# Scatter products of hops 2 to 7 as four 128x32 matrices a tile, and a table entry's low half moved one block later in the source

## The chip, the cores and the metric

One core of one Trainium2 chip runs the kernel. The metric is device time in microseconds (us) of an execution; the kernel before was timed in 3 runs with a median of 3949.62 us (3941.75 to 3951.11).

## What is computed

A graph has 10000 nodes with 128 features and 160000 random edges `src -> dst`. Seven times ("hops") each node takes the sum of its in-neighbours' features, scaled by `deg_inv_sqrt` at both ends. The eight stages of each node's features then go through a small attention block, and one row per node comes out. Cut to what matters here:

```python
h = x
toks = [x]
for _ in range(7):
    msg = h[src] * deg_inv_sqrt[src, None] * deg_inv_sqrt[dst, None]
    h = segment_sum(msg, dst, N)
    toks.append(h)
tok = stack(toks, axis=1)                    # (N, 8, D)
out = attention_readout(tok)                 # layer norm, one head, residual, softmax readout
```

## The kernel before, in words

The nodes are cut into 79 tiles of 128. Features live in a table in SBUF, `tab`, as two float16 halves per entry (a high half, columns 0 to 127, and a low half that holds the rounding error, columns 128 to 255); there are two tables, read and written in turn. The first stage sorts the edges; hop 1 also builds, for each tile of target nodes, a matrix row `w` of zeros and ones in float8 that is stored in DRAM (`GSd`) and loaded again in each of hops 2 to 7.

Hops 2 to 7 (`run`, second part) each run over 79 blocks, one for a tile `t` of target nodes, and call `block`. A block works in three steps.

- **Gather** (`gather`, L608): the edges of a tile are sorted into 72 cells of up to 32 edges, one per tile of source nodes. For each cell a product of a 128x32 matrix (a quarter of TensorE's columns, `tile_position=(0, 32 * q)`) with a table tile of 256 columns picks the 32 source rows. Four such products stand side by side and fill 128 partitions; two such groups fill one PSUM tile `p`, so a block has 9 tiles `p` and 72 products.
- **Eviction** (L613 and L615): tiles `p` 0, 2, 4, 5 and 7 are copied to SBUF (`eb`, a ring of 14) by ScalarE (ACT), tiles 1, 3, 6 and 8 by VectorE (DVE). There are 6 buffers for `p`, so tile 6 waits for the eviction of tile 0.
- **Scatter** (`scat`, L583): for each half of an `eb` tile a product of a 128x128 matrix of `w` with 256 columns adds the edges' rows into `acc`, one row per target node. There are 18 in a block.

Edges that fit in no cell are fetched row by row with an indirect DMA that POOL issues (`fetch`, L544): `og` from the table's last tiles (`tabh`), `og` of the overflow (`tabd`). Their rows go into `acc` with two more wide products (`fetched`, L568; `Sov` is the overflow's matrix). In the first two blocks of a hop the overflow's product comes last (L597, "late"). The fetch for a block is issued two blocks ahead; the first of its two DMAs stands behind a one-column copy (L543) that waits for an eviction of the block's first tile.

Scatter lags behind gather: TensorE's order in a block is 72 gather products, the two L568 products, the last 4 scatter products of the block before, then the first 14 of this one. When the last scatter product of a block is done, `close` sums the two halves of `acc` on DVE (L599, `s`), and `fin` makes the next table's entry (`entries`: the high half on ACT, L644; the low half on DVE, L645; the largest value on DVE, L646), sends the entry's rows to DRAM for the later fetches (`rows`, L168 and L172, on SP's queue), and writes the token (`token_out`: scaled by POOL, L653; sent by SP, L655).

The code is written in program order, and a scheduler then sets the order of the instructions on each engine; waits are by semaphores. In hop 1, `block` runs with `first` set and adds the halves apart (L558, L559); the change does not reach it. The attention at the end runs from an order written out by hand and is the same in both kernels.

Of the kernel before, what the change touches and what calls it, by code (L numbers as in the profile page):

```python
# [13 lines left out]
ALU = mybir.AluOpType  # L14
X = mybir.AxisListType.X
# [4 lines left out]
NT = 79  # L20
NG = 18
NI = 1
# [25 lines left out]
class Hops:  # L48
# [91 lines left out]
    def spread(self, pp, m, out, tag="acc"):  # L140
        nc = self.nc
        pb = pp.tile([128, 512], F32, name="pb", tag=tag)[:, 0:1]
        nc.tensor.matmul(pb, self.ones32, m, start=True, stop=True)
        nc.vector.tensor_copy(out, pb)
# [401 lines left out]
        return o  # L546

    def block(self, t, w, tab, og, pend, lag, runs, first, evac, fin, lead=False, late=False, mid=None, ahead=None,
              after=None):

        nc, V, A, T, G = self.nc, self.nc.vector, self.nc.scalar, self.nc.tensor, self.nc.gpsimd
        acc = []

        def both(W, rows, start, ones):

            T.matmul(acc[0][:, :128 + ones], W, rows[:, 128:256 + ones], start=start, stop=False, skip_group_check=True)  # L558
            T.matmul(acc[0][:, :128], W, rows[:, :128], start=False, stop=False, skip_group_check=True)  # L559


        def fetched(i, start=False, stop=False):
            W = w[:, (NG + i) * 128:(NG + i + 1) * 128] if i < NI else self.Sov[:, t, :]
            if first:
                both(W, og[i], False, 0)
                T.matmul(acc[0][:, 128:129], W, self.ones16, start=False, stop=stop, skip_group_check=True)  # L566
                return
            T.matmul(acc[0][:, :256], W, og[i], start=start, stop=stop)  # L568

        def begin():  # L570
            acc.append(self.pacc.tile([128, 512], F32, name="acc", tag="acc"))
            for i in range(NI if late else NI + 1):
                fetched(i, start=i == 0)

        def scat(e, jj):
            if not acc:
                acc.append(self.pacc.tile([128, 512], F32, name="acc", tag="acc"))
            for j in range(e.shape[1]):
                J = 2 * jj + j
                if first:  # L580
                    both(w[:, J * 128:(J + 1) * 128], e[:, j], J == 0, 1)
                else:
                    T.matmul(acc[0][:, :256], w[:, J * 128:(J + 1) * 128], e[:, j, :256], start=False, stop=J == NG - 1 and not late)  # L583
                if first and J == 0 and not lead:
                    for i in range(NI):
                        fetched(i)

        def close():
            if first:
                if lead:  # L590
                    for i in range(NI):
                        fetched(i)
                fetched(NI, stop=True)
                fin(t, acc[0][:, :128], acc[0])
                return
            if late:
                T.matmul(acc[0][:, :256], self.Sov[:, t, :], og[NI], start=False, stop=True)  # L597
            s = self.fp.tile([128, 128], F32, name="s")
            V.tensor_reduce(s, acc[0][:, 0:256].rearrange("p (h d) -> p d h", h=2), axis=X, op=ALU.add)  # L599
            fin(t, s, acc[0])  # L600

        def gather(jj):
            n = min(2, NG - 2 * jj)
            p = self.pg.tile([128, 2, 2, 128], F32, name="p")
            for j in range(n):
                for q in range(4):
                    s = 4 * (2 * jj + j) + q
                    T.matmul(p[32 * q:32 * q + 32, j], w[:, NJ * 128 + s * CAP:NJ * 128 + (s + 1) * CAP], tab[:, s, :], start=True, stop=True)  # L608
            e = self.ebuf[self.eb_i % len(self.ebuf)]
            self.eb_i += 1  # L610
            pv = p[:, :n].rearrange("p j h d -> p j (h d)")
            if evac(jj):
                A.activation(e[:, :n, 0:256], pv, AF.Copy, scale=4.0)  # L613
            else:
                V.tensor_tensor(e[:, :n, 0:256], pv, self.four[:, :, None].to_broadcast([128, n, 256]), op=ALU.mult)  # L615
# [24 lines left out]

    def entries(self, t, s, i):

        c, new = self.c1[i][:, t:t + 1], self.tab[1 - i]
        self.nc.scalar.activation(new[:, t, 0:128], s, AF.Copy, scale=c)  # L644
        self.nc.vector.scalar_tensor_tensor(new[:, t, 128:256], s, c, new[:, t, 0:128], op0=ALU.mult, op1=ALU.subtract)  # L645
        self.nc.vector.tensor_reduce(self.mx[1 - i][:, t:t + 1], new[:, t, 0:128], axis=X, op=ALU.max, apply_absolute_value=True)  # L646

    def token_out(self, k, t, s, ct):
        r = self.fp.tile([128, 128], F32, name="r")
# [7 lines left out]
    def run(self, ctx, att, nhop=K):  # L657
        tc, nc, V, A, T, G = self.tc, self.nc, self.nc.vector, self.nc.scalar, self.nc.tensor, self.nc.gpsimd
        with ExitStack() as c:
# [35 lines left out]
            dsl, W = [[] for _ in quads], [[] for _ in quads]  # L695
# [30 lines left out]
        with ExitStack() as c:  # L726
# [11 lines left out]
            for k in range(2, nhop + 1):  # L738
                i = 1 - k % 2
# [20 lines left out]

                def fin(t, s, acc, k=k, ct=ct, last=last, i=i):
                    if not last:
                        self.entries(t, s, i)
                        self.rows(1 - i, self.tab[1 - i], t, t + 1, nc.sync)
                    self.token_out(k, t, s, ct)


                order = [*range(4 * NG, NT), *range(4 * NG)]
# [12 lines left out]
                for n, t in enumerate(order):  # L781
                    w = self.gsp.tile([128, (NJ + NG) * 128], F8, name="w")
                    nc.sync.dma_start(w, self.GSd[t])
                    if k == 2 and n == 20:
                        att.constants(c, self.pg.tile([128, 512], F32, name="aw", tag="p"), self.ident)
                    if last and 40 <= n < 40 + 8 * FIRST:
                        att.load((n - 40) // 8, (n % 8,))

                    after = pend.pop() if n == 1 else None
                    for _ in self.block(t, w, tab, og[n], pend, 2, (9,), False, lambda jj: jj in (0, 2, 4, 5, 7), fin, n == 0, n < 2,  # L790
                                        (lambda part, n=n: scale(part, n)) if n < 2 and not last else None,
                                        lambda after=None, n=n: ahead(n, after), after):
                        pass
                while pend:
                    pend.pop(0)()
# [578 lines left out]
```

## Time and profile before

| | us |
|---|---|
| median of 3 runs | 3949.62 |
| lowest, highest | 3941.75, 3951.11 |
| the profiled execution | 3958.33 |
| its span (first to last instruction) | 3956.4 |
| TensorE busy | 3707.2 |
| VectorE busy | 3165.6 |
| ScalarE busy | 2812.9 |
| POOL busy | 1689.8 |
| granted TensorE clock, mean | 0.974 |

Engines are named PE (TensorE's products), PEld (its weight loads), DVE, ACT, POOL and SP. "128*32" in a row is the matrix, "128x256" the moving operand. In a timeline each row is a run of equal instructions: start, duration, engine, line, what is written and read, how many, and in brackets how long the engine sat idle before and what ended it. In a chain each row is a stretch of the path that ended last.

### The profile page before, as it was taken

To read this page: it belongs to the slowest core of one execution; us is meant where nothing else is said; L and a number is where in the kernel's file an instruction comes from. 1 tells how busy PE (TensorE), PEld (TensorE's weight loads), DVE (VectorE), ACT (ScalarE), POOL (GpSimd) and SP (SyncE) were. 2 spreads that over 40 slices of the span, in tenths; PEclk is the share of its full clock that TensorE was granted. 3 is DMA by queue.
4 is the path that set the end of the run, shared out by engine and by line. 5 is a ranking of instruction groups with operands and counts; after the bars stand their busy time and mean duration, and the time that the engine had idled before them with its cause. 6 is when DMAs were issued, how large, how long until landed. Compare 5 with 4: busy or idle time off the path is not lost.

```text
span 3956.4 us, 174256 instructions
## 1 busy us (share of the span) xinstructions
PE 3707.2 (94%) x74141; PEld 2992.0 (76%) x74141; DVE 3165.6 (80%) x6888; ACT 2812.9 (71%) x6950; POOL 1689.8 (43%) x2221
## 2 busy tenths in 40 slices
PE   6787899999989999999999999999999998999997
PEld 4665677777768888888888788878878886777775
DVE  8998999998867777777777777777776664888888
ACT  6885577777776666766667677666765657888885
POOL 0000234333345665666566566656656662121111
PEclk8998899999999999999999999999999999999998
DMA  3100454545456666666666666666666653222220
GB/s 101 37 2 1 146 160 152 164 148 158 142 160 191 199 202 194 203 200 203 192 198 203 183 205 203 198 191 198 203 191 202 189 183 98 83 76 84 77 83 18
DMA packets 332729, 595.58 MB, mean 151 GB/s; under 512 B 57447, under 2 KB 215493, under 8 KB 326693
## 3 DMA queue, kind: packets, MB, share of 16 engines
q1 hardware_dynamic: 293989, 506.70, 40.6%
q0 software_dynamic: 35392, 72.55, 6.7%
q8 instruction: 580, 9.50, 1.0%
q10 hardware_dynamic: 2560, 5.12, 0.5%
q14 instruction: 208, 1.70, 0.2%
HBM read 455.49 MB, written 128.67 MB: 148 GB/s over the span
## 4 chain that ended last, share of the span: by engine, by line
PE 72%; DVE 16%; DMA 5%; ACT 3%; issue 2%; SPq 1%; another core or an unknown queue 0%; ACTq 0%; DVEq 0%; POOLq 0%
PE p L608 26%; PE acc L583 23%; PE acc L568 4%; PE pv L1018 4%; PE pu L1002 3%; DMA rb<-srow 2%; DVE o L219 2%; DVE w L532 2%; DVE oh L213 2%; DVE ux L226 2%; PE po L1037 2%; PE tb L449 2%; PE pt L992 2%; PE ps L1067 1%; ACT rs L347 1%
## 5 line engine op out<-in xcount | busy, mean ns | idle before, releaser
L613 ACT ACTIVATE eb<-p 128x512 f16<-128x512 f32 x3065 | 1636.7, 604 | 566.2 <-PE p L608 327.9
L615 DVE TENSOR_TENSOR eb<-p,four 128x512 f16<-128x512 f32 x1912 | 1232.0, 686 | 334.8 <-PE acc L583 201.3
L608 PE MATMUL p<-tab,w 128*32 128x256 f16 x39816 | 1296.2, 275 | 42.8 <-issue 15.3
L608 PEld LDWEIGHTS <-w 128*32 128x32 fp8e4 x39816 | 998.9, 96 | 231.6 <-issue 171.4
L583 PE MATMUL acc<-eb,w 128*128 128x256 f16 x8532 | 1013.6, 273 | 0.7 <-issue 0.7
L583 PEld LDWEIGHTS <-w 128*128 128x128 fp8e4 x8532 | 836.7, 98 | 99.9 <-issue 1.3
L544 POOL DMA_INDIRECT og<-tabh,oidx x553 | 626.1, 1132 | 662.3 <-DVE vi L487 388.3
L544 POOL DMA_INDIRECT og<-tabd,oidx x541 | 553.4, 1023 | 752.2 <-PE acc L566 311.8
L653 POOL TENSOR_SCALAR r<-s,ctok 128x128 f32<-128x128 f32 x474 | 294.9, 622 | 48.7 <-DVE s L599 31.1
L644 ACT ACTIVATE tab<-s,c 128x128 f16<-128x128 f32 x395 | 158.5, 401 | 204.0 <-DVE eb L615 167.7
L645 DVE SCALAR_TENSOR_TENSOR tab<-s,c,tab 128x128 f16<-128x128 f32 x395 | 138.9, 352 | 180.6 <-issue 168.8
L1107 POOL TENSOR_TENSOR p<-e,in 128x1024 f32<-128x1024 f32 (+1 forms) x40 | 76.5, 1913 | 447.0 <-DVE e L1106 447.0
L1059 ACT ACTIVATE junk<-tab 128x128 f32<-128x128 f32 x626 | 248.6, 402 | 8.4 <-SPq L1343 6.8
L347 ACT ACTIVATE rs<-iof,rb 128x128 fp8e4<-128x128 f32 x784 | 231.8, 389 | 0.3
L599 DVE TENSOR_REDUCE s<-acc 128x128 f32<-128x256 f32 x474 | 196.8, 415 | 24.8 <-PE acc L597 11.7
L558 PE MATMUL acc<-eb,w 128*128 128x129 f16 x1422 | 214.5, 225 | 1.8 <-ACT eb L613 1.7
L532 DVE TENSOR_TENSOR w<-dsl,iof 128x2432 fp8e4<-128x2432 f16 x79 | 211.9, 2683 | 0.8 <-PE acc L559 0.8
L559 PE MATMUL acc<-eb,w 128*128 128x128 f16 x1422 | 210.7, 222 | 0.0
L558 PEld LDWEIGHTS <-w 128*128 128x128 fp8e4 x1501 | 140.1, 98 | 65.8 <-issue 62.9
L543 POOL COPY og<-eb 128x1 f16<-128x1 f16 x452 | 84.1, 186 | 240.2 <-ACT eb L613 240.1
L1018 PEld LDWEIGHTS pv<-Wv,xT 128*64 128x64 f32 x2504 | 138.9, 137 | 44.7 <-ACT uT L1003 29.1
L1018 PE MATMUL pv<-Wv,xT 128*64 128x131 f32 x2504 | 163.6, 280 | 8.4 <-issue 4.6
(299 smaller groups left out, 5048.7 us busy)
## 6 DMA issues: line engine op xcount, KB each, us to landing
w<-gsd SPq DMA_DIRECT2D x474, 592.0 KB
gsd<-w SPq DMA_DIRECT2D x79, 592.0 KB
tok<-r SPq DMA_DIRECT2D x546, 64.0 KB
tab<-tok SPq DMA_DIRECT2D x273, 128.0 KB
tabd<-tab SPq DMA_DIRECT2D x396, 64.0 KB
ra<-srow SPq DMA_DIRECT2D x79, 320.0 KB
rb<-srow SPq DMA_DIRECT2D x79, 256.0 KB
og<-tabh,oidx POOLq DMA_INDIRECT x553
```

The lines of the kernel that those rows point to most:

```text
L347: A.activation(ro[:, j - a, i, :], self.iof, AF.Abs_reciprocal_sqrt, scale=2.0 ** 21, bias=rb[:, j - VP, i:i + 1], saturate=False)
L532: V.tensor_tensor(w[:, :NJ * 128].rearrange("p (j d) -> p j d", d=128), dsl[:, g, :, None].to_broadcast([128, NJ, 128]), self.iof1[:, None ...
L544: self.nc.gpsimd.indirect_dma_start(out=o, out_offset=None, in_=src[0] if i == NI else src[1], in_offset=bass.IndirectOffsetOnAxis(ap=self ...
L558: T.matmul(acc[0][:, :128 + ones], W, rows[:, 128:256 + ones], start=start, stop=False, skip_group_check=True)
L559: T.matmul(acc[0][:, :128], W, rows[:, :128], start=False, stop=False, skip_group_check=True)
L583: T.matmul(acc[0][:, :256], w[:, J * 128:(J + 1) * 128], e[:, j, :256], start=False, stop=J == NG - 1 and not late)
L608: T.matmul(p[32 * q:32 * q + 32, j], w[:, NJ * 128 + s * CAP:NJ * 128 + (s + 1) * CAP], tab[:, s, :], start=True, stop=True)
L613: A.activation(e[:, :n, 0:256], pv, AF.Copy, scale=4.0)
L615: V.tensor_tensor(e[:, :n, 0:256], pv, self.four[:, :, None].to_broadcast([128, n, 256]), op=ALU.mult)
L653: self.nc.gpsimd.tensor_scalar(r, s, ct[:, t:t + 1], None, op0=ALU.mult)
L1018: T.matmul(p[64 * h:64 * h + 64, u - us[0], :], S[i]["xT"][:, h * m + q, 64 * c:64 * c + 64], Wv, start=True, stop=True, tile_position=(0, ...
L1059: A.activation(j, S[i]["x"][:, g, :], AF.Square, bias=S[i]["x"][:, g, 0:1], scale=-1.0, accum_out=R[i % 6][:, 0, g:g + 1])
```

## The change

Two edits. In hops 2 to 7 each 128x128 product into `acc` (L568, L583, L597) becomes four products of 128x32, each with a quarter of the matrix's columns, the same 256 moving columns, and a quarter of `acc`'s partitions. And `entries` returns the making of the low half, of the largest value and of the rows' DMA as a function, which `fin` calls when the next block ends (for the last block of a hop, at once).

```diff
+            spread(W, og[i], start, stop)
+        def spread(W, rows, start, stop):
+            if not self.narrow:
+                T.matmul(acc[0][:, :256], W, rows, start=start, stop=stop)
+                return
+            for q in range(4):
+                T.matmul(acc[0][32 * q:32 * q + 32, :256], W[:, 32 * q:32 * q + 32], rows, start=start, stop=stop,
+                         tile_position=(0, 32 * q))
...
-                    T.matmul(acc[0][:, :256], w[:, J * 128:(J + 1) * 128], e[:, j, :256], start=False, stop=J == NG - 1 and not late)
+                    spread(w[:, J * 128:(J + 1) * 128], e[:, j, :256], False, J == NG - 1 and not late)
...
-                T.matmul(acc[0][:, :256], self.Sov[:, t, :], og[NI], start=False, stop=True)
+                spread(self.Sov[:, t, :], og[NI], False, True)
...
         self.nc.scalar.activation(new[:, t, 0:128], s, AF.Copy, scale=c)
-        self.nc.vector.scalar_tensor_tensor(new[:, t, 128:256], s, c, new[:, t, 0:128], op0=ALU.mult, op1=ALU.subtract)
-        self.nc.vector.tensor_reduce(self.mx[1 - i][:, t:t + 1], new[:, t, 0:128], axis=X, op=ALU.max, apply_absolute_value=True)
+        def rest():
+            self.nc.vector.scalar_tensor_tensor(new[:, t, 128:256], s, c, new[:, t, 0:128], op0=ALU.mult, op1=ALU.subtract)
+            self.nc.vector.tensor_reduce(self.mx[1 - i][:, t:t + 1], new[:, t, 0:128], axis=X, op=ALU.max, apply_absolute_value=True)
+            self.rows(1 - i, new, t, t + 1, self.nc.sync)
+        return rest
...
                     if not last:
-                        self.entries(t, s, i)
-                        self.rows(1 - i, self.tab[1 - i], t, t + 1, nc.sync)
+                        rest.append(self.entries(t, s, i))
                     self.token_out(k, t, s, ct)
+                    while len(rest) > (t != order[-1]):
+                        rest.pop(0)()
```

On TensorE, in the middle of a hop, these rows stood where gathers end and scatter begins (`og0` and `og1` are the fetched rows, `eb6` and `eb7` evicted tiles of the block before):

```order
L568 LDWEIGHTS w_48618
L568 MATMUL acc_48715<-og0_48376,w_48618 128x256
L568 LDWEIGHTS Sov_254
L568 MATMUL acc_48715<-og1_48379,Sov_254 128x256
L583 LDWEIGHTS w_48491
L583 MATMUL acc_48588<-eb6_24209,w_48491 128x256
```

In the change the first of these pairs is four, and so is each that follows (L576 is the new helper's product):

```order
L576 LDWEIGHTS w_63990
L576 MATMUL acc_64087<-og0_63628,w_63990 32x256
L576 LDWEIGHTS w_63990
L576 MATMUL acc_64087<-og0_63628,w_63990 32x256
L576 LDWEIGHTS w_63990
L576 MATMUL acc_64087<-og0_63628,w_63990 32x256
L576 LDWEIGHTS w_63990
L576 MATMUL acc_64087<-og0_63628,w_63990 32x256
```

A block has 152 pairs of load and product on TensorE now, where it had 92, all of them 128x32.

On VectorE, in a block in the middle of a hop, before:

```order
L615 TENSOR_TENSOR eb1_258<-p_60773,four_222 128x2x256
L615 TENSOR_TENSOR eb3_262<-p_60793,four_222 128x2x256
L599 TENSOR_REDUCE s_60810<-acc_60676 128x128
L645 SCALAR_TENSOR_TENSOR tab1_65<-s_60810,c10_24185,tab1_65 128x128
L646 TENSOR_REDUCE mx1_249<-tab1_65 128x1
```

And in the change, in the same place (L609 is the sum, L657 the low half, L658 the largest value):

```order
L625 TENSOR_TENSOR eb1_258<-p_77918,four_222 128x2x256
L625 TENSOR_TENSOR eb3_262<-p_77938,four_222 128x2x256
L609 TENSOR_REDUCE s_77973<-acc_77761 128x128
L657 SCALAR_TENSOR_TENSOR tab1_65<-s_77973,c10_24185,tab1_65 128x128
L658 TENSOR_REDUCE mx1_249<-tab1_65 128x1
```

The low half still reads the `s` that was summed just before it, of its own block: the scheduler has put it back where it stood, in all 395 cases.

On SP's queue, in the middle of a hop, before (`w` is the next matrix row, `tabd1` the entry's rows, `tok3` the token):

```order
L783 DMA w_37292<-gsd16_103 128x4736
L168 DMA tabd1_167<-tab1_65 128x256
L655 DMA tok3_68<-r_36894 128x128
L783 DMA w_37419<-gsd17_104 128x4736
L168 DMA tabd1_167<-tab1_65 128x256
```

And in the change:

```order
L799 DMA w_43397<-gsd16_103 128x4736
L670 DMA tok3_68<-r_42774 128x128
L168 DMA tabd1_167<-tab1_65 128x256
L799 DMA w_43584<-gsd17_104 128x4736
L670 DMA tok3_68<-r_42961 128x128
```

The entry's rows now stand behind the token, where they stood ahead of it.

More of the change, by code (lines that the diff above doesn't have):

```diff
@@ L548, in block @@
     def block(self, t, w, tab, og, pend, lag, runs, first, evac, fin, lead=False, late=False, mid=None, ahead=None,
-              after=None):
+              after=None, narrow=False):
         nc, V, A, T, G = self.nc, self.nc.vector, self.nc.scalar, self.nc.tensor, self.nc.gpsimd
@@ L567, in fetched @@
                 return
-            T.matmul(acc[0][:, :256], W, og[i], start=start, stop=stop)
+            spread(W, og[i], start, stop)
[6 more added lines that the diff above has]
+                         tile_position=(0, 32 * q))
         def begin():
+            self.narrow = narrow
             acc.append(self.pacc.tile([128, 512], F32, name="acc", tag="acc"))
@@ L762, in fin @@
                     if not last:
-                        self.entries(t, s, i)
-                        self.rows(1 - i, self.tab[1 - i], t, t + 1, nc.sync)
+                        rest.append(self.entries(t, s, i))
                     self.token_out(k, t, s, ct)
-                order = [*range(4 * NG, NT), *range(4 * NG)]
+                    while len(rest) > (t != order[-1]):
+                        rest.pop(0)()
+                order, rest = [*range(4 * NG, NT), *range(4 * NG)], []
                 og = [[None] * (NI + 1) for _ in order]
@@ L791, in run @@
                                         (lambda part, n=n: scale(part, n)) if n < 2 and not last else None,
-                                        lambda after=None, n=n: ahead(n, after), after):
+                                        lambda after=None, n=n: ahead(n, after), after, True):
                         pass
```

## The prediction

> **What bounds the kernel now.** I read the page's first part and its chain first, then the stretch that holds hops 2 to 7, then the chain in order of time inside one block, then the timeline of that block.
>
> ```profile
> PE 3707.2 (94%) x74141; PEld 2992.0 (76%) x74141; DVE 3165.6 (80%) x6888; ACT 2812.9 (71%) x6950; POOL 1689.8 (43%) x2221
> PE 72%; DVE 16%; DMA 5%; ACT 3%; issue 2%; SPq 1%; another core or an unknown queue 0%; ACTq 0%; DVEq 0%; POOLq 0%
> ...
> 1196.00:3305.00 2109.00, 2084.95 (x43408) 1755.13 (x43399) 1584.15 (x3206) 1408.74 (x2754) 1302.34 (x1864) 1.00 0.63 196
> ```
>
> The last row is the stretch of hops 2 to 7 (columns: PE, PEld, DVE, ACT, POOL, granted clock, DMA share, GB/s). TensorE is busy in 2084.95 of 2109 us at full clock, and VectorE, the next, in 1584.15 (75%). The chain there is TensorE alone:
>
> ```profile
> 2003.51 0.32 PE acc L568 x2
> 2003.84 1.97 PE acc L583 x18
> 2005.80 2.08 PE p L608 x72
> 2007.88 0.33 PE acc L568 x2
> ```
>
> A block of 128 target nodes takes 2007.88 - 2003.51 = 4.37 us: 2 products of fetched rows (L568), 18 scatter products (L583), and 18 groups of four gather products (L608). A scatter product takes 1.97/18 = 0.1094 us. Eighteen gather groups at that pace would take 1.97, and they take 2.08: 0.11 too much. Two L568 products would take 0.22, and they take 0.32: 0.10 too much. Both surpluses stand where TensorE changes between 128x128 and 128x32 matrices. This is what the change can remove: **0.21 us a block**.
>
> What TensorE meets once it runs 128x32 matrices alone is read from the timeline of the same block.
>
> ```profile
> 2003.00 1.02 POOL L544 DMA_INDIRECT og<-tabh,oidx  x1 [0.27 <-POOL og L543]
> 2003.67 2.13 PE L583 MATMUL acc<-eb,w 128*128 128x256 f16 x18
> 2004.42 0.60 ACT L613 ACTIVATE eb<-p 128x512 f16<-128x512 f32 x1 [0.47 <-PE acc L583]
> 2004.45 0.69 DVE L615 TENSOR_TENSOR eb<-p,four 128x512 f16<-128x512 f32 x1 [0.46 <-PE acc L583]
> 2004.76 0.95 POOL L544 DMA_INDIRECT og<-tabd,oidx  x1 [0.74 <-PE acc L583]
> 2005.06 0.41 DVE L599 TENSOR_REDUCE s<-acc 128x128 f32<-128x256 f32 x1
> 2005.51 0.40 ACT L644 ACTIVATE tab<-s,c 128x128 f16<-128x128 f32 x1 [0.49 <-DVE s L599]
> 2005.73 2.15 PE L608 MATMUL p<-tab,w 128*32 128x256 f16 x72
> 2005.94 0.35 DVE L645 SCALAR_TENSOR_TENSOR tab<-s,c,tab 128x128 f16<-128x128 f32 x1 [0.47 <-issue]
> 2006.24 2.06 ACT L613 ACTIVATE eb<-p 128x512 f16<-128x512 f32 x4 [0.34 <-PE p L608]
> ```
>
> POOL issues two indirect gathers a block, at 2003.00 and 2004.76. The gather products ended by the chain at 2003.51, yet ACT and DVE get the last two tiles only at 2004.42 and 2004.45, 0.40 us after POOL's instruction was over (2003.00 + 1.02), though both had been idle for 0.47 and 0.46. So news that TensorE has finished is held while POOL issues. The wide scatter products run through it without a gap (18 in 2.13 us, 0.27 of it the last one's depth). In a few blocks POOL is late and its issue falls into the gather products. There narrow products do stop:
>
> ```profile
> 1314.77 1.38 PE L608 MATMUL p<-tab,w 128*32 128x256 f16 x43
> 1314.86 0.94 POOL L544 DMA_INDIRECT og<-tabd,oidx  x1 [0.31 <-DMA tabd<-tab]
> 1316.40 0.60 PE L608 MATMUL p<-tab,w 128*32 128x256 f16 x13 [0.24 <-issue]
> ...
> 2023.20 1.38 PE L608 MATMUL p<-tab,w 128*32 128x256 f16 x42
> 2023.29 0.95 POOL L544 DMA_INDIRECT og<-tabd,oidx  x1 [0.30 <-issue]
> 2024.84 0.62 PE L608 MATMUL p<-tab,w 128*32 128x256 f16 x14 [0.26 <-issue]
> ...
> 2977.38 1.38 PE L608 MATMUL p<-tab,w 128*32 128x256 f16 x44
> 2977.61 0.95 POOL L544 DMA_INDIRECT og<-tabd,oidx  x1 [0.30 <-issue]
> 2979.10 0.56 PE L608 MATMUL p<-tab,w 128*32 128x256 f16 x12 [0.34 <-issue]
> ```
>
> These are the first, one from the middle and the last of six such blocks, and I found no block in which 40 narrow products stood behind a POOL issue and no stop came. The stop comes after 40 to 46 products, in the middle of a tile, on an instruction that waits for no semaphore. In the first, 43 products at 0.1094/4 take 1.18 us; the next starts 1.63 after the stretch did: 0.45 lost. The six lose 0.45, 0.51, 0.49, 0.48, 0.62 and 0.52, **0.51 on average**. My reading is that while POOL issues, TensorE's finished products are not signed off, and that some 33 to 40 may be open at once: 3.6 us of work or more in wide products, 0.9 to 1.1 us in narrow ones.
>
> **The change, part by part.**
>
> *Switches removed.* 0.21 us in each block whose gathers and scatters meet.
>
> ```profile
> L568 PE MATMUL acc<-og,w x474: 271/283/395, 1185.2 to 3301.3; 128*128 128x256 f16 x158
> ```
>
> There are 474 blocks; in the first two of each of the six hops TensorE waits for other things, so I count 462: 462 x 0.21 = 97 us off.
>
> *Products added.* 20 wide products become 20 groups of four, 60 more load-and-product pairs a block. No row shows a narrow product that adds to acc; the nearest rows are the gathers, whose group takes 2.08/18 = 0.1156 us with the switch in it, and 0.1094 if the surplus is the switch's. So 20 groups cost between nothing and 20 x 0.006 = 0.12 us a block more. A gain has no source, since 256 rows still stream per group. I take nothing, because the group's four products stream side by side in the gathers. Whether loads or issue could hold them back:
>
> ```profile
> L608 PEld LDWEIGHTS <-w 128*32 128x32 fp8e4 x39816 | 998.9, 96 | 231.6 <-issue 171.4 <-ACT w L529 5.2 <-DMA tok<-r 0.6
> L1067 PE MATMUL ps<-xT,uT 128*32 128x32 f32 x5008 | 56.2, 199 | 1.8 <-issue 1.6 <-ACT uT L1003 0.2
> q8 instruction: 580, 9.50, 1.0%
> ```
>
> The attention's small products are done at 56.2/5008 = 0.011 us each, against 0.027 wanted here, so issue is fast enough while nothing holds it. The instruction queue carries 9.50 MB for 2 x 74141 TensorE instructions; 56,880 more are 3.6 MB, at 0.63 DMA share, beside other work. A narrow load takes 96 ns, but four go side by side, or a gather group could not take 0.12. [...]
>
> *POOL's issue now meets narrow products always.* At 2003.00 and 2004.76 it lay beside wide products that hid it. That cover is gone in both places. Bounds for what one meeting costs: nothing (the wide case, if scatter products, which fewer engines wait for, are held less) and 0.62 (the worst of the six). I take 0.51, since the six are narrow products at the same pace. Two per block: +1.02 us. The first starts behind the copy that waits for the block's first eviction, and hits the last gathers and the scatter; the second starts when the fetched rows' buffer is given back, and hits the end of the scatter. In the six blocks a second loss followed (the first tiles' evictions came late); here the two places are later in the block, so I count none. [...]
>
> *Low half.* The source makes it a block later, but the instruction order of the change has VectorE's multiply (L645, now L657) straight behind the reduction of its own block in all 395 cases, as before. So its 0.47 us wait for ACT stays; DVE at 1584 of 2109 us hides it. On SP the token's row is now issued ahead of the table's rows. Inside a hop nobody waits for either. At the five hop ends the next hop's fetch waits for the last table rows:
>
> ```profile
> 1535.43 0.60 POOL L653 TENSOR_SCALAR r<-s,ctok 128x128 f32<-128x128 f32 x1 [1.19 <-DVE s L599]
> 1536.16 0.35 DVE L645 SCALAR_TENSOR_TENSOR tab<-s,c,tab 128x128 f16<-128x128 f32 x1
> 1536.54 0.32 SPq L168 DMA_DIRECT2D tabd<-tab  x1
> 1536.96 0.38 SPq L655 DMA_DIRECT2D tok<-r  x1
> ```
>
> The token's data is ready at 1536.03 and its issue takes 0.38, so it is out of the way before 1536.54: between nothing and 0.4 us, five times. I take nothing.
>
> *Sum.* -0.21 + 1.02 = +0.81 us in 462 blocks: +374 us, a block of 5.18. The profiled execution took 3958.33 us (span 3956.4), 8.7 over the median of 3949.62; from there the sum gives 4333, against the median **4325 us**.
>
> **Rivals.**
>
> *No stop in the scatter (faster).* The held thing could be the news alone, and the stop a matter of gathers. Then TensorE needs 38 groups x 0.1094 = 4.16 us a block. For it: wide products never stopped. Against it: the stops come in the middle of tiles, on products that nobody waits for, which scatter products resemble. It decides if fewer than some 33 products are open when POOL ends. Price: -0.21 x 474 = -100, 3850 us.
>
> *The news as a chain (a little faster).* Without a stop, POOL's two issues, the evictions and the copy form a ring: eviction at 2006.24, copy, first issue, buffer given back, second issue (ends 2005.71 in the row above), next eviction 0.53 later. The shortest wait seen from the end of an issue to an eviction is the 0.40 of 2004.42, so the ring needs at least 4.37 - 0.13 = 4.24 us, and at most the 4.37 it has. Middle 4.30, -0.07 x 462 = -32, 3918 us.
>
> *One meeting only.* If the second issue finds nothing to hold, because no one waits for the late scatter products: -0.21 + 0.51 = +0.30, 4088 us.
>
> *The change gains and costs nothing:* narrow groups at 0.1156 for all 38 are 4.39 us a block, +0.02 x 474 = 10 us, 3959 us; it needs the surplus to belong to narrow groups and not to the switch. Against it: L568, wide, shows the same surplus.
>
> **How the numbers follow.** Both meetings 0.52, one meeting 0.10, nothing 0.04, ring 0.08, no stop 0.26. About 0.3% (12 us) is what a measurement of this kernel can tell from no change. Faster 0.34, same 0.04, slower 0.62. The forecast's own range takes 0.45 to 0.62 a meeting and up to 0.12 for the groups: 462 x (0.90 - 0.21) = +319 to 462 x (1.24 + 0.12 - 0.21) = +531, so 4269 to 4480. Leaving out the no-stop case would leave out more than 2 in 10, so the range goes from 3845 to 4480.
>
> **What would show it.** Right: in hops 2 to 7 TensorE's rows break about 1.1 us behind each POOL issue, with some 0.5 us idle put down to "issue"; a block in the chain is near 5.2 us; DVE and ACT are busy for a smaller share. The switch is judged apart: between L608 and L568 no surplus over 0.109 us. Wrong: rows unbroken through POOL's issue and a block of 4.16 (no stop), or breaks that end with an eviction and a block of 4.3 (ring). If the evictions of the last two tiles no longer lag behind POOL's issue, my reading of the hold is wrong from the start.

## The result, and the profile after

| | 128x128 scatter (before) | 128x32 scatter (after) |
|---|---|---|
| median of four runs, us | 3949.39 | 4389.81 (4379.69 to 4393.82) |
| ratio, 95% interval | | 1.1119 [1.1105, 1.1134] |
| profiled execution, us (span) | 3958.33 (3956.4) | 4386.04 (4384.1) |
| TensorE busy, us (share of the span) | 3707.2 (94%) | 3826.0 (87%) |
| TensorE products | 74141 | 102581 |

The change makes the kernel 11% slower; 4325 was forecast. The page of after, its first part and its chain by engine:

```profile
PE 3826.0 (87%) x102581; PEld 3167.3 (72%) x102581; DVE 3185.8 (73%) x6888; ACT 2808.6 (64%) x6950; POOL 1687.5 (38%) x2221
PE 69%; DVE 14%; issue 9%; DMA 4%; ACT 4%; SPq 0%; ACTq 0%; DVEq 0%
```

"issue" has grown from 2% to 9% of the chain: time in which TensorE waits for nothing that the profile shows. One regular block in the chain in order of time:

```profile
2108.50 0.70 PE acc L576 x17
2109.20 1.97 PE p L618 x72
2111.17 0.57 PE acc L576 x21
2111.74 0.19 issue
2111.93 1.39 PE acc L576 x42
2113.32 0.37 issue
2113.69 0.71 PE acc L576 x17
```

The gathers (L618) now take 1.97 us instead of 2.08: the switches are gone. But the 80 scatter products (L576) are cut into three pieces, and the block takes 2113.69 - 2108.50 = 5.19 us instead of 4.37. Where the cuts lie is seen in the block before it, first POOL's rows in the timeline, then TensorE's:

```profile
2105.43 1.02 POOL L544 DMA_INDIRECT og<-tabh,oidx  x1 [0.27 <-POOL og L543]
2107.18 0.94 POOL L544 DMA_INDIRECT og<-tabd,oidx  x1 [0.73 <-PE acc L576]
```

```profile
2105.72 0.35 PE L576 MATMUL acc<-og,w 128*32 128x256 f16 x4
2105.83 0.35 PE L576 MATMUL acc<-og,Sov 128*32 128x256 f16 x4
2105.93 0.62 PE L576 MATMUL acc<-eb,w 128*32 128x256 f16 x14
2106.72 1.36 PE L576 MATMUL acc<-eb,w 128*32 128x256 f16 x41 [0.17 <-issue]
2108.50 0.70 PE L576 MATMUL acc<-eb,w 128*32 128x256 f16 x17 [0.41 <-issue]
```

From POOL's first issue to the first stop TensorE starts some 10 gathers (0.29 us at 0.0273) and 4 + 4 + 14 products, 32 in all; it goes on at 2106.72, 0.27 us after POOL's end (2105.43 + 1.02). The second stop ends 0.38 us after POOL's second end. A row's duration holds its last product's depth (0.27 us, the mean of one product in the page), so the bracket understates a stop; from the start of one product to that of the next, less the usual 0.027, the medians over all blocks are 0.45 for the first stop and 0.61 for the second. That is the forecast's picture, and the median of all blocks is 5.19 us. The number of open products, some 33 to 40 in the forecast's reading, is near the 32 counted at the first stop. The second stop doesn't fit it: from POOL's second issue to that stop TensorE starts the 41 products of its row less some 17 that start before 2107.18, about 24. Over all blocks the medians are 31 at the first stop and 25 at the second, so one fixed number is not shown.

But there is a second kind of stop, which I had not forecast. From the timeline some blocks later:

```profile
2126.50 1.02 POOL L544 DMA_INDIRECT og<-tabh,oidx  x1 [0.27 <-POOL og L543]
...
2127.01 0.30 PE L576 MATMUL acc<-eb,w 128*32 128x256 f16 x3
2127.92 0.60 ACT L623 ACTIVATE eb<-p 128x512 f16<-128x512 f32 x1 [0.47 <-PE acc L576]
...
2128.42 2.13 PE L576 MATMUL acc<-eb,w 128*32 128x256 f16 x69 [1.12 <-issue]
```

TensorE stops after the three products of the row at 2127.01 and stays stopped until 2128.42, 0.50 us after ACT has been told that products are finished. Nothing is held any more by then, and still it doesn't go on. 76 of 456 regular blocks (all but the first two of a hop and its end) take over 5.55 us, up to 7.44, most of them (66) for such a stop, and the mean block is 5.27.

### The profile page after: what moved, and what is told of

Read it like the earlier page. It is cut to its first block, busy times and chain, and to the rows that moved or that the text cites. A ratio compares the mean times of both kernels' runs of the same rounds, so it can differ in the third digit from the quotient of the medians.

```text
span 4384.1 us, 231134 instructions
## 1 busy us (share of the span) xinstructions
PE 3826.0 (87%) x102581; PEld 3167.3 (72%) x102581; DVE 3185.8 (73%) x6888; ACT 2808.6 (64%) x6950; POOL 1687.5 (38%) x2221
## 3 DMA queue, kind: packets, MB, share of 16 engines
q8 instruction: 803, 13.16, 1.2%
## 4 chain that ended last, share of the span: by engine, by line
PE 69%; DVE 14%; issue 9%; DMA 4%; ACT 4%; SPq 0%; ACTq 0%; DVEq 0%
PE acc L576 28%; PE p L618 23%; PE pv L1034 3%; PE pu L1018 3%; DVE w L532 2%; DMA rb<-srow 2%; PE po L1053 2%; DVE ux L226 2%; PE pt L1008 2%; DVE oh L213 2%; DVE o L219 2%; ACT rs L347 2%; PE tb L449 2%; DVE R L219 1%; PE ps L1083 1%
## 5 line engine op out<-in xcount | busy, mean ns | idle before, releaser
L576 PE MATMUL acc<-eb,w 128*32 128x256 f16 x34128 | 1250.9, 274 | 279.2 <-issue 269.2
L576 PEld LDWEIGHTS <-w 128*32 128x32 fp8e4 x36024 | 1005.4, 96 | 530.8 <-issue 520.5
L618 PE MATMUL p<-tab,w 128*32 128x256 f16 x39816 | 1319.8, 274 | 46.3 <-issue 18.5
L618 PEld LDWEIGHTS <-w 128*32 128x32 fp8e4 x39816 | 1078.2, 97 | 122.8 <-issue 74.2
L657 DVE SCALAR_TENSOR_TENSOR tab<-s,c,tab 128x128 f16<-128x128 f32 x395 | 140.2, 355 | 180.6 <-issue 142.1
L609 DVE TENSOR_REDUCE s<-acc 128x128 f32<-128x256 f32 x474 | 197.2, 416 | 82.8 <-PE acc L576 65.5
L558 PEld LDWEIGHTS <-w 128*128 128x128 fp8e4 x1501 | 139.7, 98 | 65.7 <-issue 63.1
L576 PE MATMUL acc<-og,w 128*32 128x256 f16 x1896 | 160.2, 273 | 21.5 <-issue 21.5
```

The costliest lines, as they stand in the source:

```text
L576: T.matmul(acc[0][32 * q:32 * q + 32, :256], W[:, 32 * q:32 * q + 32], rows, start=start, stop=stop, tile_position=(0, 32 * q))
```

## The experiments

Twelve kernels were run, in four groups (the first four of the table, the next four, the next three, and the last). The kernel before was timed in each group beside them, and it showed two levels, which turned out to matter: 3944 and 3955 us in two groups, like the runs above, and 3913 and 3917 in the other two.

| kernel | before, same group | us | ratio, 95% interval |
|---|---|---|---|
| narrow products alone | 3944.3 | 4393.78 | 1.1134 [1.1115, 1.1153] |
| later low half alone | 3944.3 | 3947.51 | 1.0003 [0.9994, 1.0013] |
| plain fetches, narrow | 3944.3 | 4192.93 | 1.0626 [1.0608, 1.0643] |
| plain fetches, wide | 3944.3 | 3896.56 | 0.9875 [0.9859, 0.9892] |
| fetch issued in the gathers, wide | 3912.99 | 3909.16 | 0.9995 [0.9985, 1.0004] |
| last nine scatter products narrow | 3912.99 | 4020.1 | 1.0285 [1.0267, 1.0302] |
| first nine narrow | 3912.99 | 4019.16 | 1.0281 [1.0263, 1.0298] |
| last nine narrow, plain fetches | 3912.99 | 3999.7 | 1.0231 [1.0214, 1.0249] |
| the change again | 3917.01 | 4144.97 | 1.059 [1.0551, 1.063] |
| the change, matrices once a hop | 3917.01 | 3954.23 | 1.0103 [1.0083, 1.0124] |
| plain fetches, narrow, matrices once a hop | 3917.01 | 3889.09 | 0.9936 [0.9916, 0.9956] |
| blocks in pairs, wide | 3954.68 | 4141.31 | 1.0479 [1.0461, 1.0497] |

**The two parts of the change apart.** First the narrow products without the later low half:

```diff
...
-                        rest.append(self.entries(t, s, i))
+                        self.entries(t, s, i)
+                        self.rows(1 - i, self.tab[1 - i], t, t + 1, nc.sync)
...
```

> The narrow scatter products alone; a table entry's low half, its maximum and its rows are issued in the same place as in the kernel before. POOL theory (every indirect issue of POOL holds TensorE's narrow products): the later low half does nothing, so 4390 us within 0.3% (4377 to 4403). Rival (the later low half, by the swapped order of the token and the rows on SP, is behind the longer hop ends, five of them at some 5 us): about 4365 us.

Then the later low half with 128x128 products:

```diff
-                                        lambda after=None, n=n: ahead(n, after), after, True):
+                                        lambda after=None, n=n: ahead(n, after), after, False):
```

> The later low half alone; all scatter products 128x128 as in the kernel before. POOL theory: 3949 us within 0.3% (3937 to 3961). Rival (the swapped order on SP lengthens the hop ends): about 3975 us.

4393.78 and 3947.51: all of the loss belongs to the narrow products, and the later low half does nothing that can be measured. (In the change the scheduler had put the low half itself back where it stood, so the part that is left of it is the rows' DMA behind the token's.)

**POOL's issues taken away.** Both fetches become plain transfers on SP's queue, in the narrow and in the wide kernel:

```diff
-        self.nc.gpsimd.indirect_dma_start(out=o, out_offset=None, in_=src[0] if i == NI else src[1],
-                                          in_offset=bass.IndirectOffsetOnAxis(ap=self.oidx[:, t, i:i + 1], axis=0))
+        b = t if i == NI else t % (NT - 4 * NG)
+        self.nc.sync.dma_start(o, src[0 if i == NI else 1][b * 128:b * 128 + 128, :])
```

> The changed kernel, but in hops 2 to 7 both fetched tiles of a block are read by plain transfers of 128 consecutive rows from SP's queue instead of POOL's indirect gathers (so they hold rows that the lists don't name). POOL theory: no stops, a block at 38 x 0.1094 = 4.16 us, and the time about 97 to 100 us below that of the 128x128 kernel with the same transfers, so some 3830 to 3855 us. Rival (the narrow products themselves, or the supply of their instructions, are too slow, and POOL only happens to be there): the stops stay and the time is 4300 us or more. In between, if only the rare long stops (84 blocks of over 5.5 us in the changed kernel) come from the supply of instructions: they stay, some 40 us, 3870 to 3895.

> The kernel before (128x128 scatter products), with the same plain transfers from SP's queue instead of POOL's indirect gathers in hops 2 to 7 (rows that the lists don't name). All theories: blocks stay at 4.37 us, since 128x128 products were not stopped; the few stops in gathers (nine, some 0.5 us each) go and the hop ends get shorter, so 3920 to 3950 us. If it gets far faster, POOL's issue cost the kernel before something too.

The narrow kernel comes to 4192.93, far from the 3830 to 3855 that my theory wanted and not the 4300 of the rival. The wide one, 3896.56, is 23 us below the 3920 to 3950 expected: POOL's issues cost the kernel before 48 us, more than I thought. So POOL's issues cost the narrow kernel something, and something else costs it 296 us without them. The timeline of the narrow kernel with plain fetches:

```profile
2107.16 0.12 PEld L576 LDWEIGHTS <-w 128*32 128x32 fp8e4 x4
2107.27 0.30 PE L576 MATMUL acc<-og,w 128*32 128x256 f16 x4
2107.27 0.10 PEld L576 LDWEIGHTS <-Sov 128*32 128x32 fp8e4 x1
2109.00 0.29 PE L576 MATMUL acc<-og,Sov 128*32 128x256 f16 x4 [1.44 <-issue]
2109.01 0.10 PEld L576 LDWEIGHTS <-Sov 128*32 128x32 fp8e4 x3 [1.64 <-issue]
```

It stops in the middle of a group of four: one load has been made, three come 1.7 us later. Such stops come at other places from block to block, and not with the work. What they do keep to is the product's number. Here are five stops in a row, with the packets of the instruction queue from the same trace (each is 16,384 bytes; the page has 13.16 MB in 803 of them, and 13.16 MB for 102581 products is 128 bytes a load-and-product pair, so a packet is 128 pairs):

```
packet starts   TensorE stops   goes on    pairs since the stop before
2106.72         2107.29         2109.00    128
2118.75         2119.39         2121.06    384
2127.27         2127.96         2129.65    256
2131.22         2133.05         2133.94    128
2134.99         2137.35         2137.69    128
```

Of the 375 stops of over 0.23 us between 1250 and 3200 us, 362 are at the same number modulo 128 (give or take three), and TensorE goes on 2.23 to 2.75 us after a packet's start (10 to 90%). I read this as TensorE having run out of instructions. In the changed kernel 193 of 738 stops are of this kind, 166 of 443 us; the other 545, 277 us, go with POOL's issues (some 500 of them end 0.1 to 0.55 us after the end of one), and they are gone here. In the kernel before neither kind is common: 64 stops, 38.9 us, 6 of them at a common number.

**POOL's issue moved, and half of the scatter narrow.** These four were made to tell the hold from the supply. The first leaves all scatter products wide and puts POOL's first issue next to the gathers, which are narrow anyway:

```diff
-                if jj == 0 and not first and not mid:
+                if jj == 8 and not first and not mid:
```

> The kernel before with one thing moved: POOL's copy ahead of the first fetch of a block waits for the eviction of the ninth gather tile instead of the first, so that the indirect issue starts near the next block's gathers, which are 128x32 in both kernels. All scatter products stay 128x128. POOL theory: the gather products now stop once a block for 0.45 to 0.6 us, so a block of 4.8 to 5.0 us and 4150 to 4230 us, or more if the evictions that are told late stop the gathers a second time. Supply theory (TensorE runs dry because instructions for narrow products arrive too slowly, POOL's issue has nothing to do with it): the number of products is that of the kernel before, so 3950 us.

It changed nothing. Its timeline:

```profile
2102.48 0.97 POOL L544 DMA_INDIRECT og<-tabh,oidx  x1 [0.27 <-POOL og L543]
...
2102.61 2.15 PE L608 MATMUL p<-tab,w 128*32 128x256 f16 x72
2103.13 2.55 ACT L613 ACTIVATE eb<-p 128x512 f16<-128x512 f32 x5 [0.96 <-PE p L608]
```

72 narrow products run through, and ACT gets its first tile at 2103.13, in the midst of POOL's issue: TensorE's news (the semaphore updates that tell the others that a product is done) are not held at all in this run. In the trace of the kernel before, around 2060 us, products that end 0.30 us after the start of POOL's first issue have their news 1.35 us after it; here those that end 0.54 us after it have them at 0.56. I counted over all blocks how often no news of TensorE came between 0.2 and 0.95 us after the start of POOL's first issue: in 95% of the issues in the kernel before, 87% in the change, 90% and 95% in the first two experiments; but 1% here, and 4% to 6% in the other kernels with POOL's first issue from the two groups in which the kernel before takes 3913 and 3917 us. A product with news ends in that time behind 94% to 99% of these issues, in every one of the kernels, so there was something to hold in all of them. (Behind the second issue there mostly is nothing to tell: in 4% to 10%.) So the hold belongs to some groups of runs and not to others, and this run doesn't test what it was made for. The next three are in that group as well:

```diff
...
+                    if J < 9:
+                        T.matmul(acc[0][:, :256], w[:, J * 128:(J + 1) * 128], e[:, j, :256], start=False, stop=False)
+                    else:
+                        spread(w[:, J * 128:(J + 1) * 128], e[:, j, :256], False, J == NG - 1 and not late)
```

> The changed kernel, but the fetched rows' two products and the first nine scatter products of a block are 128x128 again; only the last nine are four 128x32 each. A block then has 119 load-and-product pairs (92 before, 152 in the changed kernel), and two switches as before. POOL theory: the first issue meets the last gathers and wide products and costs nothing, the second meets the narrow end of the scatter and the next gathers: 0.5 to 0.6 us a block, 4180 to 4230 us. Supply theory (128 pairs need about 4.3 to 4.9 us): 119 pairs are supplied within 4.37 us or nearly so, 3950 to 4010 us.

> The reverse: the fetched rows' products and the first nine scatter products of a block are four 128x32 each, the last nine are 128x128. 125 pairs a block, two switches. POOL theory: the first issue meets the last gathers and the narrow half and costs 0.45 us a block, the second starts near the end of the narrow half and meets wide products: 4140 to 4180 us. Supply theory: 3950 to 4050 us.

> As the kernel with only the last nine scatter products narrow, but with plain transfers from SP's queue instead of POOL's indirect gathers (rows that the lists don't name). Its measure is the 128x128 kernel with these transfers, 3897 us. Supply theory: 119 pairs a block are nearly supplied in 4.37 us, so 3895 to 3965 us. If a narrow scatter product is slow in itself (for each one that adds to acc), about half of what all twenty cost without POOL (296 us): 4045 us. POOL theory alone: 3897.

(The rest of the edit makes the fetched rows' products 128x128 again. The second kernel has the two branches the other way round and leaves those products narrow; the third is the first with the plain fetches as well.) 4020.1, 4019.16 and 3999.7: not the hold's numbers. The first and the third are above the supply's too (3950 to 4010 and 3895 to 3965), the second lies within (3950 to 4050). The chain of the first one shows why:

```profile
2100.34 1.97 PE p L621 x72
2102.30 0.32 PE acc L568 x2
2102.62 0.55 PE acc L576 x16
2103.18 1.09 PE acc L594 x9
2104.26 0.66 PE acc L576 x20
2104.92 1.97 PE p L621 x72
```

The last four scatter products of a block are issued after the next block's gathers, so half of the scatter narrow gives four switches and not two, which I had overlooked. A block takes 2104.92 - 2100.34 = 4.58 us without any stop (4.588 is the median of all), and 38 groups at 0.1094 are 4.157: 0.43 for four switches, **0.107 us each**. Each of the four rows behind a change is 0.10 to 0.11 longer than its groups at that pace, to 128x128 (L568, L594) as to 128x32 (L576). Two more switches in 462 blocks are 99 us, and 107, 106 and 103 were lost (the last against the plain wide kernel at 3897, from another group). So these runs say nothing of either kind of stop, but they price the switch, which the prediction took from 0.21 a block.

**The change again, and with less traffic.** Two theories were left to be tested: that the held news explain the difference between groups, and that an instruction packet is late because 592 KB of matrices are loaded in each block. The second was tried by one edit, in the change and in the narrow kernel with plain fetches:

```diff
-                    w = self.gsp.tile([128, (NJ + NG) * 128], F8, name="w")
-                    nc.sync.dma_start(w, self.GSd[t])
+                    if n == 0:
+                        w = self.gsp.tile([128, (NJ + NG) * 128], F8, name="w")
+                        nc.sync.dma_start(w, self.GSd[t])
```

> The changed kernel itself, unaltered, once more: the runs of the 128x128 kernel have shown two levels (3944 to 3949 us, where TensorE's news are held in 95% of POOL's indirect issues, and 3913 us in the group of runs where they were not held). Hold theory: where the 128x128 kernel takes about 3945, this takes 4390 (ratio 1.11); where it takes about 3913, only the supply of instructions is left, and it takes 3913 + 296 = 4209 (ratio 1.075). Rival (the level has nothing to do with it): 1.11 on either level.

> The changed kernel, but in hops 2 to 7 the 592 KB of matrices are loaded once a hop instead of once a block, so all blocks of a hop use the first block's matrices. Theory: an instruction fetch is late because it queues behind these transfers; without them the stops at every 128th product go. Then with the hold a block is at 5.15 to 5.19 us with two stops of 0.45 and 0.6 (4340 to 4360 us, ratio 1.10), and without the hold it is at 4.16 (ratio 0.97 to 0.98). Rival (a fetch is always that slow): as the unaltered change.

> The narrow kernel with plain transfers instead of POOL's indirect gathers (4193 us with the matrices loaded for each block), and now with the matrices loaded once a hop: neither POOL's issues nor the 592 KB a block. Theory: no stops at all, a block at 38 x 0.1094 = 4.16 us, 3760 to 3830 us. Rival (a fetch is always that slow): the stops at every 128th product stay, 4150 to 4190 us.

The unaltered change takes 4144.97 here, 245 us less than in the first group, while the kernel before differs by 32. It loses 228 us to the kernel before of its group; the 4209 expected took the 296 of the plain fetches over. Its chain, and POOL's and TensorE's rows of a block in its timeline:

```profile
2106.00 2.12 PE acc L576 x69
2108.13 1.58 PE p L618 x59
2109.70 0.32 issue
2110.02 0.60 PE p L618 x13
2110.62 2.18 PE acc L576 x80
2112.80 1.97 PE p L618 x72
2114.76 2.18 PE acc L576 x80
```

```profile
2118.38 1.02 POOL L544 DMA_INDIRECT og<-tabh,oidx  x1 [0.27 <-POOL og L543]
...
2119.28 0.35 PE L576 MATMUL acc<-og,Sov 128*32 128x256 f16 x4
...
2119.39 2.21 PE L576 MATMUL acc<-eb,w 128*32 128x256 f16 x72
2119.91 0.94 POOL L544 DMA_INDIRECT og<-tabd,oidx  x1 [0.51 <-PE acc L576]
```

80 narrow products take 2.18 us, 0.109 a group, through both of POOL's issues. A block without a stop is 4.14 to 4.16 us. Of the 378 stops that are left 357 are at a 128th product. So both causes are real, each for its own stops. What the traffic does is read from one stretch in five kernels (the last three columns are granted clock, DMA share and GB/s): wide with plain fetches, narrow with plain fetches, the change again, the change with one load a hop, and narrow with plain fetches and one load a hop:

```profile
1250.00:3100.00 1850.00, 1849.02 (x38830) 1567.68 (x38830) 1403.48 (x2920) 1228.14 (x2488) 330.87 (x826) 1.00 0.67 202
```

```profile
1250.00:3100.00 1850.00, 1595.80 (x55607) 1486.87 (x55599) 1253.19 (x2616) 1088.84 (x2196) 287.03 (x716) 1.00 0.59 177
```

```profile
1250.00:3100.00 1850.00, 1643.77 (x57255) 1533.69 (x57251) 1309.86 (x2691) 1120.85 (x2259) 1038.66 (x1489) 1.00 0.59 182
```

```profile
1250.00:3100.00 1850.00, 1777.54 (x62634) 1674.24 (x62630) 1408.42 (x2873) 1209.59 (x2439) 1138.37 (x1631) 1.00 0.25 64
```

```profile
1250.00:3100.00 1850.00, 1815.46 (x64526) 1732.55 (x64518) 1414.80 (x2931) 1239.73 (x2500) 331.04 (x831) 1.00 0.24 66
```

The first number in brackets, TensorE's products, gives the time of a packet: 1850 us over it, times 128 (hop ends included). It is 6.10 us in the wide kernel, which needs no more; 4.26 and 4.14 in the narrow ones at a DMA share of 0.59; 3.78 and 3.67 at 0.25 and 0.24. At full pace 128 narrow products take 3.50. With less traffic packets come closer together, and the theory is right in its direction; that the stops would vanish was wrong, and 3954.23 and 3889.09 lie between what the theory and the rival wanted. In the last kernel 235 stops remain, 221 of them at the 128th product, for 93 us instead of 362, and its mean block is 4.32. That is the narrow kernel without hold, without POOL and with about a third of the traffic, and 4.34 is the mean block of the wide one with plain fetches: the change would gain next to nothing even so. (The wide kernel with one load a hop was not run.)

The packets' starts in these four traces of narrow kernels show why stops remain. A packet's own transfer takes 1.05 to 1.09 us on average in all four. Exactly one packet starts while TensorE works through 128 pairs, in all 532 rounds of the last kernel and in all but four or fewer of each of the others. Counted from the moment TensorE begins the 128, it starts after 1.72 and 1.49 us (medians; a tenth over 2.78 and 2.56) where the matrices are loaded in each block, and after 1.13 and 1.12 (a tenth over 1.85 and 1.33) with one load a hop. From its start to the next 128 are 2.4 to 2.5 us (medians) in each. So the traffic delays a packet's start and not its transfer, and even a start after 1.1 makes a round of 3.5 us, which is all that 128 narrow products take. I read the limit as this round of one packet at a time, and not as bytes per second.

**Fewer switches without more products.** If a switch costs 0.107 us and products cost supply, the version to try is the kernel before with its blocks in pairs:

```diff
...
-                begin()
+                if keep is None:
+                    begin()
+                else:
+                    pend.insert(len(pend) - 9, begin)
...
-            while len(pend) > lag:
+            while len(pend) > (lag if not keep else 99):
...
-                                        lambda after=None, n=n: ahead(n, after), after):
+                                        lambda after=None, n=n: ahead(n, after), after,
+                                        None if n < 2 else n % 2 == 0):
...
```

(The rest of the edit passes `keep` to `block` and adds buffers.)

> The kernel before (128x128 scatter products, no product added), with the blocks of a hop from the third on taken in pairs: the gathers of two blocks, 144 products of 128x32, then the scatter products of both, 40 of 128x128; eight more buffers for evicted tiles and one more of each fetched tile. So there are two switches in two blocks instead of four. Switch theory (a switch costs 0.107 us whichever way, as the blocks with four switches at 4.585 us show): a pair at 8.74 - 0.214 = 8.52 us, 231 pairs, 49 us off, ratio 0.987 to 0.989. Rival 1 (evictions: 18 gather tiles come in 3.94 us, two engines evict one in about 0.32 us, 5.8 us for 18, and six PSUM tiles lie between): TensorE waits for a free tile, 0.3 us or more a pair, so no gain or slower, ratio 1.00 to 1.03. Rival 2, where news are held: POOL's issues meet the long row of gathers and stop it once a pair, 0.5 us, +66 us, ratio 1.015 to 1.02.

4141.31, ratio 1.0479, in a group where the kernel before takes 3954.68. Its chain:

```profile
2101.55 0.54 PE acc L583 x4
...
2106.02 2.91 PE p L608 x88
2108.93 0.02 issue
2108.95 0.61 ACT eb L613
2109.56 0.04 issue
2109.60 1.48 PE p L608 x40
2111.08 0.54 PE acc L583 x4
```

The first 88 gathers are followed by an eviction and not by gathers: TensorE waits for a free PSUM tile, rival 1. A pair takes 2111.08 - 2101.55 = 9.53 us, 0.79 more than two blocks of 4.37, though two switches are gone. The price was larger than the 0.3 I put on it; in the timeline ACT also idles 0.42 us until 2108.95, behind POOL's issue at 2107.59. The news of products that end 0.29 to 1.00 us after that issue's start came only from 1.35 us on, so this run has the hold, and held news have a part in the wait, which it doesn't separate from rival 1. (No news came behind 52% of the first issues. Behind the others, nearly every second one, a single one came at some 0.58 us and the next after 1.35.) Of the versions that fetch the listed rows and load every matrix, none beats the kernel before.

## Why the prediction was right, and where it was not

**Switches removed, -0.21 a block: right.** The gathers take 1.97 instead of 2.08 us, and four switches in other kernels cost 0.43.

**Products added, nothing: right while nothing stops them** (80 in 2.18 us).

**POOL's issues, two meetings of 0.51: right in mechanism for this group of runs, and in size for the typical block.** The medians are 0.45 and 0.61, 1.06 against 1.02, and the median block is 5.19 against 5.18. But not every block has both stops, and some of the second ones are at a packet's end: the 277 us of stops that go with POOL's issues are 0.77 for each of the 361 blocks between 1250 and 3200 us. What the prediction did not say, because the one trace before could not show it, is that the hold is not there in every group of runs: the same kernel takes 4390 with it and 4145 without.

**"Issue is fast enough while nothing holds it", and the instruction queue's 3.6 MB "beside other work": this step failed.** I compared an engine's rate (0.011 us a product in the attention, in rows of at most 128 products, so one packet's worth) and a total of bytes, and neither is the limit. What counts is the time from one packet of 128 pairs to the next while 592 KB a block are loaded beside it: 4.1 to 4.3 us, where narrow products need one every 3.5. Without hold or POOL this alone makes a block 4.86 (the change again) or 5.01 (plain fetches) instead of 4.16. In the run that was forecast it is 166 us in those 361 blocks, 0.46 each, a term that I had put at nothing.

**The sum came out by luck: the two losses hide each other.** The hold alone would give 5.18 and the supply alone 4.86 to 5.01; added to 4.16 that would be 5.88 to 6.03, and the mean block is 5.27; as I read it, though no run shows it apart, packets arrive while TensorE is stopped for the other reason. So removing POOL's issues gives back 197 us (4390 to 4193), of which the wide kernel gets 48 as well, and not the 1.02 x 462 = 471 put on them. The profiled executions differ by 427.7 us. 456 regular blocks went from 4.357 to 5.274 on average: +418. Of that, 0.81 a block, 369 us, was forecast; 0.08 a block, 37 us, is what the mean lies over the median, the tail of long stops; the other 12 are that the typical block grew by 0.82 and that the mean before lay 0.01 under its median. The five hop ends went from 11.4 to 16.3 us (10.35 in the change again, without the hold), +25, where five indirect issues follow each other at 1.25 us and TensorE starts four products at a time between them; I had priced only a swapped transfer there. The first two blocks of the hops and the rest of the kernel give back 15.

**Low half, nothing: right** (1.0003, and 4394 against 4390).

**The rivals.** "No stop in the scatter" was priced at 3850. What it asks for, no stop through POOL's issues, is met in the third group, and there the change takes 4145, 6% more than the kernel before: the 0.26 I gave to it rested on the step that failed. The ring and the single meeting did not show.

**What stays open:** why news of TensorE are held during POOL's indirect issue in some groups of runs and not in others. The chip alone doesn't decide it: the third group (not held) and the last one (held) both ran on the chip with number 9. That the level of the kernel before goes with it (3944 to 3955 and 3913 to 3917) fits the 38.9 us of stops in its trace, but no trace of it without the hold was taken; the nearest, with the fetch moved, has 24 stops, 14 us. A narrow kernel with the hold and without the late packets was not run in a group that had it, so the hold's price alone is read from stops in the trace and not from a time.

## What to carry to other kernels

Before one wide product is split into four, count the instructions as a stream: here 128 load-and-product pairs were one packet of 16,384 bytes, one packet came while the one before was used up, and it came every 4.1 to 4.3 us beside some 180 GB/s of traffic and every 3.7 to 3.8 us beside 65, where narrow products need one every 3.5. Two losses together cost less here than their sum (a mean block of 5.27 us against 5.88 to 6.03), so a forecast can hit the sum with one cause missing, and only taking that cause away shows it. And where one trace shows a hold, ask whether it belongs to the kernel or to the runs: the kernel timed beside each experiment gave it away.

## What the runs showed of the hardware that was not expected

- In the narrow kernel with plain fetches 362 of 375 stops of TensorE fell on the same number of load-and-product pairs modulo 128, and TensorE went on 2.23 to 2.75 us after the start of a 16,384-byte packet of the instruction queue. With DMA share 0.59 one came every 4.14 to 4.26 us on average, with 0.24 still every 3.67, though its own transfer took 1.05 to 1.09 us; it started 1.12 to 1.72 us (medians) after TensorE began the 128 pairs before, later with more traffic.
- A change between 128x128 and 128x32 matrices cost 0.107 us on average, in either direction and in each of the four places of a block (four in 4.58 us, each 0.10 to 0.11).
- TensorE's news were held while POOL issued an indirect gather in some groups of runs (no news within 0.2 to 0.95 us in 87% to 95% of the first issues; in the pairs 52%, with a single one in the others) and passed in others (1% to 6%), on one chip number both.
